# Agent attention with a mixture of experts: two left tiles under way at a time

## The chip, the cores and the metric

The kernel runs on one core of a Trainium2 chip. The metric is the device time of one execution in microseconds (us), the median over several runs. The engines are named as in the profile: PE is the matrix engine (PEld its weight loads), ACT, DVE and POOL are the scalar, vector and general engines, SP issues most of the transfers. SBUF is the on-chip memory from which the engines read, PSUM the small memory of eight banks into which PE writes.

## The reference

Four batches (B = 4) of N = 11456 tokens with C = 128 channels go through an attention by way of 49 agents, and the result, token by token, through the one of E = 8 experts (hidden width F = 1024) that a gate chooses:

```
s1 = softmax(scale * agents @ k.T);  agent_v = s1 @ v
x  = softmax(scale * q @ agents.T) @ agent_v          # N x 128, per batch
e  = argmax(x @ w_gate);  g = softmax(x @ w_gate)[e];  m = sigmoid((x @ w_output_gate)[e])
out = g * m * (relu(x @ w1[e]) @ w2[e])
```

All inputs and outputs are 32-bit floats.

## The kernel before

In each batch one expert has almost all tokens. The **main stream** sends every token of a batch through that expert, in tiles of up to 512 tokens, with 16-bit operands. `mm1` issues a group of eight matmuls `h` (four of its own weights and four of the rest) into PSUM banks 0 to 3; `relu` makes from each bank the two 16-bit parts `hh` (ACT) and `hl` (DVE); `mm2` multiplies them in pairs, one matmul with `hh` and one with `hl`, into a bank `y`; `finish` reads `y` with ACT (`ys`) and DVE (`os`), and `store` writes it out. The matmuls `ks`, `av`, `qs` of the attention, and `lg` of the gate, are put between those of the stream.

The tokens that chose another expert are gathered into **left tiles** of 128 tokens: thirteen from batches 0 to 2 (phase 0) and one from batch 3 (phase 1). They are computed again with their own expert, in 32-bit matmuls, and scattered over the result. `left_prepare` makes the table of tiles and gathers the tokens' attention rows (SP loads of indices, POOL's indirect transfers into `big` or `left_ld`). For each tile, `left_load` loads with SP the agents' values `lav` and the expert's two weight matrices `lw1`, `lw2` of 512 KB each; `left_front` transposes the tokens (`let`, copied by ACT to `let_sb`) and multiplies them with `lav` (`lx`, copied by ACT to `lxs`); `left_back` makes eight matmuls `lh` in two halves of four, each half in one bank and with one ACT relu behind it, then eight matmuls `ly`, and ACT scales the result into its place. A 32-bit matmul shows as two passes in the trace. `left_scatter` then writes the tile with a POOL transfer.

What comes when is settled while the program is built: a planner (class `Clock`) keeps an estimated time for each engine, and the generators (the main stream and the side streams, each with a priority given to `spawn`) hand out their next instruction when the planner thinks its operands ready. `wait_free` asks for a free PSUM bank, `bank` takes the one that is free longest by the planner's time. On the chip every engine works through its list in order and waits on semaphores. Loads of `k`, `q`, `v` and `x` use buffers `ld0` and on (`place` takes one, `scored` gives it back), 128 x 1024 numbers each.

In the kernel before, `left_static` works on one left tile at a time, while the loads and the front of the next one may run ahead:

```
for i, (ph, k) in enumerate(todo):
    while (ph, k) not in ready or i > finished[0] + 1:
        yield None
```

Of the kernel before, what the change touches and what calls it, by code (L numbers as in the profile page):

```python
# [7 lines left out]
F32 = mybir.dt.float32  # L8
# [8 lines left out]
P = 128  # L17
B, N, C, A, E, F = 4, 11456, 128, 49, 8, 1024
A2 = 50
# [233 lines left out]
def agent_attention_top1_moe(ctx, tc, qT, kT, v, aT, wg, wo, w1, w2, cst, out):  # L253
# [245 lines left out]
    def scored(item):  # L499
        places[held.pop(item)][0] = True  # L500
# [92 lines left out]
    def v_weights(b, u):  # L593

        base, pp, nt = UNITS[u]
        S, M = K[b]["S"], K[b]["M"]
        sv = S[0:pp, 8 * u:8 * u + nt, :]

        if b > 0:
            e = wk.tile([P, 8, A2], F32, name=f"ev{b}_{u}", tag="ev", bufs=2)  # L600
        else:
            e = wk.tile([P, 4, C], F32, name=f"ev{b}_{u}", tag="os", bufs=4).rearrange("p t c -> p (t c)")
            e = e[:, 0:8 * A2].rearrange("p (t a) -> p t a", a=A2)
        e = e[0:pp, 0:nt, :]
        yield from (DVE if b == 0 and u % 3 == 0 else POOL).q.tensor_tensor(e, sv, M[0:pp].unsqueeze(1).broadcast_to([pp, nt, A2]), op=ALU.subtract)
        yield from ACT.q.activation(e, e, AF.Exp, scale=SCALE)
        K[b][u] = e
        spawn(v_sum(b, u, e), 1)
# [714 lines left out]
            yield from pause(1500.0 if n > 1 else 0.0)  # L1323
        return ti, tg, ef, oa

    def left_load(ph, ti, k, nm):
        b0, nb, _, _ = PHASES[ph]
        yield from SY.wait(ti)
        er = nc.values_load(ti[0:1, k, 3:4], engines=[SP], min_val=0, max_val=E - 1,
                            skip_runtime_bounds_check_because=WHY)  # L1330
        yield from SY.wait(ti)
        br = nc.values_load(ti[0:1, k, 4:5], engines=[SP], min_val=0, max_val=nb - 1,
                            skip_runtime_bounds_check_because=WHY)
        av = wk.tile([P, C], F32, name=f"lav{nm}", tag="l_av")
        yield from SY.q.dma_start(av[0:A], avnd[b0:b0 + nb][bass.ds(br, 1)].rearrange("a p c -> p (a c)"))
        w1t = wk.tile([P, F], F32, name=f"lw1{nm}", tag="w1t", bufs=2)
        yield from SY.q.dma_start(w1t, w1[bass.ds(er, 1)].rearrange("a p f -> p (a f)"))
        w2t = wk.tile([P, F], F32, name=f"lw2{nm}", tag="w2t", bufs=2)
        yield from SY.q.dma_start(w2t, w2[bass.ds(er, 1)].rearrange("a p f -> p (a f)"))
        return av, w1t, w2t  # L1340

# [6 lines left out]
    def left_front(nm, ef, av):  # L1348
        yield from wait_free()
        t = bank(f"let{nm}")  # L1350
        mark = hold()
        yield from PE.q.transpose(t[0:A, 0:P], ef[:, 0:A], idf)
        et = wk.tile([P, P], F32, name=f"let_sb{nm}", tag="l_et", bufs=1)
        yield from ACT.q.copy(et[0:A], t[0:A, 0:P])
        release(mark)
        yield from wait_free()
        x = bank(f"lx{nm}")
        mark = hold()
        yield from PE.q.matmul(x[:, 0:P], av[0:A], et[0:A], start=True, stop=True)
        xs = wk.tile([P, P], F32, name=f"lxs{nm}", tag="l_xs")  # L1360
        yield from ACT.q.copy(xs, x[:, 0:P])
        release(mark)
        return xs

    def left_back(nm, xs, w1t, w2t, o, ef):
        hidden = []
        for hf in range(2):
            yield from wait_free()
            h = bank(f"lh{nm}_{hf}")
            mark = hold()  # L1370
            for j in range(4):
                fs = slice((4 * hf + j) * P, (4 * hf + j + 1) * P)
                yield from PE.q.matmul(h[:, j * P:(j + 1) * P], w1t[:, fs], xs, start=True, stop=True)
            hs = wk.tile([P, 512], F32, name=f"lh{nm}_{hf}", tag=f"lh{hf}", bufs=1)
            hidden.append(hs)
            yield from ACT.q.activation(hs, h, AF.Relu)
            release(mark)
# [13 lines left out]
                                in_=o, in_offset=None, bounds_check=top - 1, oob_is_err=False)  # L1391

    left = []

    ready = {}

# [18 lines left out]
                    ready[ph, i + k] = t, ti, k, tu[:, k:k + 1], ef[:, k, :], oa[:, k, :]  # L1415
                yield from left_index(ph, i, n, f"s{ph}_{i}", got, big)

    def left_static():
        todo = [(ph, k) for ph, x in enumerate(PHASES) for k in range(x[2])]
        ops = {}  # L1420

        def fronts():
            for i, (ph, k) in enumerate(todo):
                while (ph, k) not in ready or i > finished[0] + 1:
                    yield None
                t, ti, kk, _, ef, _ = ready[ph, k]
                yield from pause(t - clk.now())
                av, w1t, w2t = yield from left_load(ph, ti, kk, f"{ph}_{k}")
                yield from pause(max(clk.ready[x.name] for x in (av, w1t, w2t)) - clk.now())
                xs = yield from left_front(f"{ph}_{k}", ef, av)  # L1430
                ops[ph, k] = xs, w1t, w2t

        finished = [0]
        spawn(fronts(), 4)
        for ph, k in todo:
            while (ph, k) not in ops:
                yield None
            xs = ops.pop((ph, k))
            _, _, _, tu, ef, oa = ready[ph, k]
            yield from left_back(f"{ph}_{k}", *xs, oa, ef)  # L1440
            left.append((ph, oa, tu))
            finished[0] += 1

# [32 lines left out]
    spawn(clear(), 5)  # L1476
    spawn(small_products(), 4)
    spawn(left_prepare(), 1)
    spawn(left_static(), 5)
    spawn(left_scatter(), 3)  # L1480
    main_stream()

# [67 lines left out]
```

## Time and profile before

| what | value |
|---|---|
| median of 3 runs | 1042.22 us (1041.47 to 1042.23) |
| profiled execution | 1041.4 us, span 1039.6 us |
| mean granted clock of PE | 0.997 |
| PE busy | 1018.5 us (98%) |
| PEld busy | 835.1 us (80%) |
| DVE busy | 880.2 us (85%) |
| ACT busy | 589.8 us (57%) |
| POOL busy | 272.9 us (26%) |

The busy times are those of the profiled execution; its own time is 1.8 us longer than its span. All instructions carry the same line number, that of a helper, so that rows are told apart by the names of their operands, in which numbers are left out. PE's busy time counts a matmul from its start to its modelled end, and matmuls overlap.

### The profile page before, as it was taken

The numbers are of one execution on the slowest core, as the hardware profiler recorded it, in microseconds if no ns is written. First come the engines' busy times: TensorE is split into PE (matmuls) and PEld (weight loads), VectorE is DVE, ScalarE is ACT, GpSimd is POOL, SyncE is SP. The second block draws the span as 40 slices with busy tenths as digits, with TensorE's granted clock in tenths as the row PEclk, the third lists the DMA queues.
The fourth block names the chain that finished last, engine by engine and source line by source line (L and its number), as shares of the span: only waits on it lengthen the run. The fifth ranks groups of instructions, "written<-read, shape, count | busy, mean of one in ns | idle before, by whom it ended". The sixth has DMA issues, their size and how long they took to land.

```text
span 1039.6 us, 27765 instructions
## 1 busy us (share of the span) xinstructions
PE 1018.5 (98%) x10690; PEld 835.1 (80%) x10690; DVE 880.2 (85%) x2390; ACT 589.8 (57%) x1396; POOL 272.9 (26%) x442
## 2 busy tenths in 40 slices
PE   9999999999999999999999999999999999999996
PEld 9998877888688878887788888877687687878785
DVE  1748999999998999989998999889999988868851
ACT  1326665656655566565655665565755566565552
POOL 0301323332112222222122232321122333434322
PEclk9999999999999999999999999999999999999998
DMA  8877765544459445453569544444333445442441
GB/s 273 244 181 241 179 134 145 129 139 132 125 139 210 135 127 121 120 165 99 135 159 181 156 124 112 132 146 119 114 101 71 125 97 152 143 134 68 147 145 60
DMA packets 109111, 147.14 MB, mean 142 GB/s; under 512 B 61420, under 2 KB 71840, under 8 KB 108974
## 3 DMA queue, kind: packets, MB, share of 16 engines
q1 hardware_dynamic: 107630, 143.83, 50.8%
q0 software_dynamic: 1344, 1.49, 0.8%
q8 instruction: 85, 1.39, 0.6%
q14 instruction: 52, 0.43, 0.2%
HBM read 91.86 MB, written 35.17 MB: 122 GB/s over the span
## 4 chain that ended last, share of the span: by engine, by line
PE 82%; DVE 13%; ACT 3%; issue 2%; POOL 0%; DMA 0%; POOLq 0%; DVEq 0%; ACTq 0%
PE y L203 40%; PE h L203 17%; DVE hl L203 6%; PE ks L203 6%; PE av L203 6%; PE qs L203 4%; PE lh L203 2%; PE ly L203 2%; ACT hh L203 1%; PE aw L203 1%; PE warm L203 1%; DVE os L203 1%; PE lg L203 1%; DVE ll L203 1%; DVE cum L203 1%
## 5 line engine op out<-in xcount | busy, mean ns | idle before, releaser
L203 PE MATMUL y<-vv,hh 128*128 128x256 f16 (+1 forms) x2880 | 588.3, 273 | 4.7 <-DVE qz L203 3.0
L203 PE MATMUL y<-vv,hl 128*128 128x128 f16 (+1 forms) x2880 | 530.3, 219 | 1.4 <-DVE hl L203 0.7
L203 ACT ACTIVATE hh<-h 128x512 f16<-128x512 f32 (+1 forms) x736 | 372.3, 591 | 203.5 <-PE h L203 203.2
L203 DVE SCALAR_TENSOR_TENSOR hl<-h,hh 128x512 f16<-128x512 f32 (+1 forms) x736 | 446.7, 666 | 44.8 <-ACT hh L203 42.3
L203 PEld LDWEIGHTS <-hh 128*128 128x128 f16 (+1 forms) x2880 | 283.3, 98 | 65.0 <-issue 36.1
L203 PEld LDWEIGHTS <-hl 128*128 128x128 f16 (+1 forms) x2880 | 322.3, 112 | 7.5 <-DVE hl L203 4.0
L203 PE MATMUL h<-x_ld,w 128*128 128x512 f16 (+1 forms) x1472 | 283.9, 376 | 2.4 <-DVE hl L203 1.7
L203 POOL TENSOR_TENSOR os<-os,smt 128x512 f32<-128x512 f32 (+1 forms) x92 | 94.0, 1022 | 299.5 <-issue 224.3
L203 PEld LDWEIGHTS <-w 128*128 128x128 f16 x1472 | 97.2, 103 | 88.7 <-issue 67.5
L203 PEld LDWEIGHTS qs<-at,q_ld 128*128 128x128 f32 x720 | 112.8, 191 | 7.9 <-DVE os L203 0.6
L203 PE MATMUL qs<-at,q_ld 128*128 128x50 f32 x720 | 114.2, 245 | 0.1
L203 ACT COPY ys<-y 128x256 f32<-128x256 f32 x180 | 67.7, 376 | 76.8 <-PE y L203 76.7
L203 PE MATMUL av<-ev,v_ld 128*128 128x50 f32 x720 | 109.7, 251 | 0.0
L203 PEld LDWEIGHTS av<-ev,v_ld 128*128 128x128 f32 x720 | 107.7, 192 | 2.3 <-issue 0.8
L203 PE MATMUL ks<-at,k_ld 128*128 128x50 f32 x720 | 107.9, 256 | 0.4 <-DVE os L203 0.4
L203 PEld LDWEIGHTS ks<-at,k_ld 128*128 128x128 f32 x720 | 104.6, 191 | 2.8 <-DVE os L203 1.6
L203 DVE TENSOR_TENSOR os<-y,ys 128x256 f32<-128x256 f32 x180 | 74.4, 413 | 22.0 <-ACT ys L203 19.3
L203 POOL TENSOR_TENSOR e<-ef,e 128x392 f16<-128x392 f32 (+1 forms) x48 | 41.4, 862 | 156.8 <-ACT e L203 136.6
L203 POOL TENSOR_TENSOR ev<-S,km_o 128x400 f32<-128x400 f32 (+1 forms) x44 | 40.5, 922 | 119.7 <-PE av L203 56.8
L203 PEld LDWEIGHTS <-idle_x 128*128 128x128 f16 x324 | 47.6, 154 | 3.1 <-DVE idle_x L203 1.1
L203 DVE TENSOR_REDUCE m<-ks 128x50 f32<-128x400 f32 (+1 forms) x44 | 23.8, 540 | 25.4 <-ACT S L203 25.0
L203 ACT COPY S<-ks 128x400 f32<-128x400 f32 (+1 forms) x48 | 22.7, 476 | 36.4 <-PE ks L203 36.3
(228 smaller groups left out, 1055.2 us busy)
## 6 DMA issues: line engine op xcount, KB each, us to landing
q_ld<-qT SPq DMA_DIRECT2D x44, 512.0 KB
v_ld<-v SPq DMA_DIRECT2D x44, 512.0 KB
out<-os SPq DMA_DIRECT2D x88, 256.0 KB
k_ld<-kT SPq DMA_DIRECT2D x43, 512.0 KB
lw<-w SPq DMA_DIRECT2D x28, 512.0 KB
efd<-ef SPq DMA_DIRECT2D x44, 200.0 KB
x_ld<-x_ld SPq DMA_DIRECT2D x176, 38.0 KB
w1t<-w SPq DMA_DIRECT2D x8, 256.0 KB
```

The lines of the kernel that those rows point to most:

```text
L203: return getattr(self.eng, op)(*a, **k)
```

## The change

Two generators `left_static(way)` take every other left tile each. A way loads the weights of its next tile only when its previous tile is done. The weights go to the buffers of the loads (`left_place`) and no longer to `w1t` and `w2t`. The second way starts when all values of the last batch are loaded, and its hidden layer lies in the buffers of the tag `ev`, whose shape is made to fit. `let_sb` gets a second buffer.

```diff
@@ -597,7 +597,8 @@
         sv = S[0:pp, 8 * u:8 * u + nt, :]
 
         if b > 0:
-            e = wk.tile([P, 8, A2], F32, name=f"ev{b}_{u}", tag="ev", bufs=2)
+            e = wk.tile([P, 4, C], F32, name=f"ev{b}_{u}", tag="ev", bufs=2).rearrange("p t c -> p (t c)")
+            e = e[:, 0:8 * A2].rearrange("p (t a) -> p t a", a=A2)
         else:
             e = wk.tile([P, 4, C], F32, name=f"ev{b}_{u}", tag="os", bufs=4).rearrange("p t c -> p (t c)")
             e = e[:, 0:8 * A2].rearrange("p (t a) -> p t a", a=A2)
@@ -1323,7 +1324,7 @@
             yield from pause(1500.0 if n > 1 else 0.0)
         return ti, tg, ef, oa
 
-    def left_load(ph, ti, k, nm):
+    def left_load(ph, ti, k, nm, at_=None):
         b0, nb, _, _ = PHASES[ph]
         yield from SY.wait(ti)
         er = nc.values_load(ti[0:1, k, 3:4], engines=[SP], min_val=0, max_val=E - 1,
@@ -1333,9 +1334,15 @@
                             skip_runtime_bounds_check_because=WHY)
         av = wk.tile([P, C], F32, name=f"lav{nm}", tag="l_av")
         yield from SY.q.dma_start(av[0:A], avnd[b0:b0 + nb][bass.ds(br, 1)].rearrange("a p c -> p (a c)"))
-        w1t = wk.tile([P, F], F32, name=f"lw1{nm}", tag="w1t", bufs=2)
+        if at_ is None:
+            w1t = wk.tile([P, F], F32, name=f"lw1{nm}", tag="w1t", bufs=2)
+        else:
+            w1t = yield from at_(f"lw1{nm}")
         yield from SY.q.dma_start(w1t, w1[bass.ds(er, 1)].rearrange("a p f -> p (a f)"))
-        w2t = wk.tile([P, F], F32, name=f"lw2{nm}", tag="w2t", bufs=2)
+        if at_ is None:
+            w2t = wk.tile([P, F], F32, name=f"lw2{nm}", tag="w2t", bufs=2)
+        else:
+            w2t = yield from at_(f"lw2{nm}")
         yield from SY.q.dma_start(w2t, w2[bass.ds(er, 1)].rearrange("a p f -> p (a f)"))
         return av, w1t, w2t
 
@@ -1350,7 +1357,7 @@
         t = bank(f"let{nm}")
         mark = hold()
         yield from PE.q.transpose(t[0:A, 0:P], ef[:, 0:A], idf)
-        et = wk.tile([P, P], F32, name=f"let_sb{nm}", tag="l_et", bufs=1)
+        et = wk.tile([P, P], F32, name=f"let_sb{nm}", tag="l_et")
         yield from ACT.q.copy(et[0:A], t[0:A, 0:P])
         release(mark)
         yield from wait_free()
@@ -1362,7 +1369,7 @@
         release(mark)
         return xs
 
-    def left_back(nm, xs, w1t, w2t, o, ef):
+    def left_back(nm, xs, w1t, w2t, o, ef, tag="lh"):
         hidden = []
         for hf in range(2):
             yield from wait_free()
@@ -1371,7 +1378,7 @@
             for j in range(4):
                 fs = slice((4 * hf + j) * P, (4 * hf + j + 1) * P)
                 yield from PE.q.matmul(h[:, j * P:(j + 1) * P], w1t[:, fs], xs, start=True, stop=True)
-            hs = wk.tile([P, 512], F32, name=f"lh{nm}_{hf}", tag=f"lh{hf}", bufs=1)
+            hs = wk.tile([P, 512], F32, name=f"lh{nm}_{hf}", tag=tag, bufs=2)
             hidden.append(hs)
             yield from ACT.q.activation(hs, h, AF.Relu)
             release(mark)
@@ -1391,6 +1398,8 @@
                                 in_=o, in_offset=None, bounds_check=top - 1, oob_is_err=False)
 
     left = []
+    WAYS, LEFT = 2, 5
 
     ready = {}
 
@@ -1415,29 +1424,41 @@
                     ready[ph, i + k] = t, ti, k, tu[:, k:k + 1], ef[:, k, :], oa[:, k, :]
                 yield from left_index(ph, i, n, f"s{ph}_{i}", got, big)
 
-    def left_static():
-        todo = [(ph, k) for ph, x in enumerate(PHASES) for k in range(x[2])]
+    def left_place(nm):
+        while not vacant():
+            yield None
+        return place((nm, 0, 0), first_place(0, LARGE)[1], [F])
+    def left_static(way):
+        while way and (B - 1 not in K or K[B - 1]["v"] < NU):
+            yield None
+        todo = [(ph, k) for ph, x in enumerate(PHASES) for k in range(x[2])][way::WAYS]
         ops = {}
+        finished = [0]
 
         def fronts():
             for i, (ph, k) in enumerate(todo):
-                while (ph, k) not in ready or i > finished[0] + 1:
+                while (ph, k) not in ready or i > finished[0]:
                     yield None
                 t, ti, kk, _, ef, _ = ready[ph, k]
                 yield from pause(t - clk.now())
-                av, w1t, w2t = yield from left_load(ph, ti, kk, f"{ph}_{k}")
+                av, w1t, w2t = yield from left_load(ph, ti, kk, f"{ph}_{k}", left_place)
                 yield from pause(max(clk.ready[x.name] for x in (av, w1t, w2t)) - clk.now())
                 xs = yield from left_front(f"{ph}_{k}", ef, av)
                 ops[ph, k] = xs, w1t, w2t
 
-        finished = [0]
-        spawn(fronts(), 4)
+        spawn(fronts(), LEFT - 1)
         for ph, k in todo:
             while (ph, k) not in ops:
                 yield None
             xs = ops.pop((ph, k))
             _, _, _, tu, ef, oa = ready[ph, k]
-            yield from left_back(f"{ph}_{k}", *xs, oa, ef)
+            yield from left_back(f"{ph}_{k}", *xs, oa, ef, ("lh", "ev")[way])
+            for x in (f"lw1{ph}_{k}", f"lw2{ph}_{k}"):
+                scored((x, 0, 0))
             left.append((ph, oa, tu))
             finished[0] += 1
 
@@ -1476,7 +1497,8 @@
     spawn(clear(), 5)
     spawn(small_products(), 4)
     spawn(left_prepare(), 1)
-    spawn(left_static(), 5)
+    for way in range(WAYS):
+        spawn(left_static(way), LEFT)
     spawn(left_scatter(), 3)
     main_stream()
 
```

The order that the planner makes of it is the same on every engine up to about 816 us, and the last left tile (phase 1) stands alone behind the last `y` of the main stream in both kernels. In between, the rows of the left tiles stand elsewhere in the same stream. Two places follow. Names end in the tile's number, and the number of a half where there is one; `w` stands for the main stream's first weights, `vv` for its second.

The first place is where the sixth and seventh left tiles (`_5` and `_6`) meet, near 921 us, on PE, now:

```order
L203 MATMUL h_0_3_17389<-x_7_ld,w_0_13705 128x512 [waits DMAHW3_49]
L203 MATMUL qs_11_17383<-at,q_11_ld 96x50
L203 MATMUL lh_6_0_17368<-lxs_6_17354,lw_60_0_ld 128x128 x3
L203 MATMUL ly_5_17388<-lw_50_0_ld,lh_5_0_17327 128x128 [waits DMAHW3_49,DVE_49]
L203 MATMUL ly_5_17388<-lw_50_0_ld,lh_5_0_17327 128x128
L203 MATMUL lh_6_1_17428<-lxs_6_17354,lw_60_0_ld 128x128 [waits Activation_49]
L203 MATMUL lh_6_1_17428<-lxs_6_17354,lw_60_0_ld 128x128 x3
L203 LDWEIGHTS hh_0_17186
L203 MATMUL y_0_17441<-vv_0_13690,hh_0_17186 128x256 [waits Activation_49]
```

Before, behind the same group of `h` on PE:

```order
L203 MATMUL h_0_3_17366<-x_7_ld,w_0_13705 128x512
L203 LDWEIGHTS hh_2_17180
L203 MATMUL y_0_17323<-vv_0_13690,hh_2_17180 128x256
L203 MATMUL lh_5_0_17348<-lxs_5_17333,lw_5_17156 128x128 [waits DMAHW4_49,Activation_49]
L203 LDWEIGHTS hl_2_17181
L203 MATMUL y_0_17323<-vv_0_13690,hl_2_17181 128x128
```

The `lh` and `ly` of two tiles now stand side by side without main matmuls between them, and a new `y` behind them waits for ACT. On ACT the same place reads now:

```order
L203 COPY ys_1_17374<-y_1_17249 128x256 [waits PE_49,Activation_49]
L203 ACTIVATE lh_5_1_17373<-lh_5_1_17342 128x512 [waits PE_49]
L203 ACTIVATE hh_0_17395<-h_0_0_17370 128x512 [waits PE_49]
L203 ACTIVATE hh_1_17398<-h_0_1_17376 128x512 [waits PE_49]
L203 ACTIVATE hh_2_17400<-h_0_2_17385 128x512 [waits PE_49]
L203 ACTIVATE hh_3_17402<-h_0_3_17389 128x512 [waits PE_49]
L203 ACTIVATE lh_6_0_17420<-lh_6_0_17368 128x512 [waits PE_49]
L203 ACTIVATE lh_6_1_17436<-lh_6_1_17428 128x512 [waits PE_49]
```

In the kernel before, the relus of one tile stood there:

```order
L203 COPY lxs_5_17333<-lx_5_17310 128x128 [waits PE_49]
L203 ACTIVATE hh_0_17372<-h_0_0_17350 128x512 [waits PE_49]
L203 ACTIVATE hh_1_17375<-h_0_1_17353 128x512 [waits PE_49]
L203 ACTIVATE hh_2_17377<-h_0_2_17357 128x512 [waits PE_49]
L203 ACTIVATE hh_3_17379<-h_0_3_17366 128x512 [waits PE_49]
L203 ACTIVATE ef_11_17391<-qz_11_17383 96x2x49 [waits DMAHW4_49,DVE_49,Pool_49]
L203 ACTIVATE lh_5_0_17409<-lh_5_0_17348 128x512 [waits PE_49]
L203 CAST e_3_86<-ef_11_17391 96x2x49 [waits DMAHW5_49,Activation_49]
L203 ACTIVATE lh_5_1_17436<-lh_5_1_17416 128x512 [waits PE_49]
```

The relu `lh_6_0` stands directly behind the four `hh` of the group, ahead of the second half's.

The second place is where the ninth and tenth tiles (`_8` and `_9`) meet, near 970 us, on PE, now; ahead of these rows stand, from the `h` group on, eight pairs of `y` with a `pexc` (a small product of the table of tiles) and `let_8` in the first two:

```order
L203 LDWEIGHTS hh_7_18131
L203 MATMUL y_1_18271<-vv_1_13692,hh_7_18131 128x256
L203 LDWEIGHTS hl_7_18132
L203 MATMUL y_1_18271<-vv_1_13692,hl_7_18132 128x128
L203 MATMUL let_9_18351<-kc,big_8_17075 49x128 [waits DMASW6_49,Activation_49]
L203 MATMUL lx_8_18345<-let_sb_8_18326,lav_8_18174 128x128 [waits DMAHW5_49,PE_49]
L203 LDWEIGHTS w_1_13721
L203 MATMUL h_0_0_18358<-x_9_ld,w_1_13721 128x512 [waits DVE_49]
```

The transposition `let_9` stands between two groups of `h`, and waits for ACT; before, one `let` stood further on between `y` pairs, and no second. On ACT, now:

```order
L203 ACTIVATE hh_4_18310<-h_1_0_18296 128x512 [waits PE_49]
L203 ACTIVATE hh_5_18313<-h_1_1_18298 128x512 [waits PE_49]
L203 ACTIVATE hh_6_18315<-h_1_2_18301 128x512 [waits PE_49]
L203 ACTIVATE hh_7_18317<-h_1_3_18304 128x512 [waits PE_49]
L203 COPY let_sb_8_18326<-let_8_18303 49x128 [waits PE_49]
L203 COPY ys_1_18347<-y_1_18271 128x256 [waits DVE_49,PE_49]
L203 COPY let_sb_9_18353<-let_9_18351 49x128 [waits PE_49]
L203 COPY lxs_8_18355<-lx_8_18345 128x128 [waits PE_49]
```

And before:

```order
L203 ACTIVATE hh_4_18289<-h_1_0_18265 128x512 [waits PE_49]
L203 ACTIVATE hh_5_18292<-h_1_1_18267 128x512 [waits PE_49]
L203 ACTIVATE hh_6_18294<-h_1_2_18281 128x512 [waits PE_49]
L203 ACTIVATE hh_7_18296<-h_1_3_18283 128x512 [waits PE_49]
L203 COPY ys_1_18326<-y_1_18238 128x256 [waits DVE_49,PE_49]
L203 ACTIVATE hh_0_18369<-h_0_0_18352 128x512 [waits PE_49]
```

The copies of the two transpositions now stand behind `hh_4` to `hh_7`, and `let_9` takes the bank that `let_sb_8` reads.

## Rows read from the trace of the kernel before

**Rows 1.** The page: the span, and the chain of waits by engine.
```profile
span 1039.6 us, 27765 instructions
...
PE 82%; DVE 13%; ACT 3%; issue 2%; POOL 0%; DMA 0%; POOLq 0%; DVEq 0%; ACTq 0%
```

**Rows 2.** Stretches: length; busy PE, PEld, DVE, ACT, POOL; clock, DMA share, GB/s.
```profile
836.00:1025.00 189.00, 189.00 (x1888) 155.90 (x1887) 143.41 (x419) 106.35 (x258) 66.75 (x89) 1.00 0.42 126
1025.00:1040.00 15.00, 5.04 (x41) 4.42 (x39) 0.49 (x2) 2.53 (x7) 2.67 (x3) 0.81 0.04 12
```

**Rows 3.** Groups of PE from 836 to 1025 us: count, busy, mean, idle.
```profile
L203 PE MATMUL y<-vv,hh 128*128 128x256 f16 (+1 forms) x541 | 113.9, 273 | 0.0
...
L203 PE MATMUL h<-x_ld,w 128*128 128x512 f16 (+3 forms) x264 | 51.7, 374 | 0.0
L203 PE MATMUL ly<-lw,lh 128*128 128x128 f32 x208 | 40.1, 275 | 0.0
L203 PE MATMUL lh<-lxs,lw 128*128 128x128 f32 x200 | 38.7, 275 | 0.0
```

**Rows 4.** Timeline of PE near 915 us: start, duration, engine, instruction.
```profile
914.94 1.35 PE L203 MATMUL h<-x_ld,w 128*128 128x512 f16 x8
916.23 0.28 PE L203 MATMUL y<-vv,hh 128*128 128x256 f16 x1
...
917.23 0.27 PE L203 MATMUL y<-vv,hh 128*128 128x256 f16 x1
...
917.50 0.27 PE L203 MATMUL y<-vv,hh 128*128 128x256 f16 x1
...
917.66 0.27 PE L203 MATMUL y<-vv,hh 128*128 128x256 f16 x1
...
918.99 0.27 PE L203 MATMUL y<-vv,hh 128*128 128x256 f16 x1
...
921.78 0.27 PE L203 MATMUL y<-vv,hh 128*128 128x256 f16 x1
...
922.17 0.27 PE L203 MATMUL y<-vv,hh 128*128 128x256 f16 x1
```

**Rows 5.** Timeline near 835 us; in brackets idle time and releaser.
```profile
834.63 0.60 ACT L203 ACTIVATE lh<-lh 128x512 f32<-128x512 f32 x1 [0.27 <-PE lh L203]
...
835.28 0.27 PE L203 MATMUL y<-vv,hh 128*128 128x256 f16 x1 [0.54 <-ACT lh L203]
```

**Rows 6.** Timeline of PE and ACT near 921 us.
```profile
921.38 0.28 PE L203 MATMUL y<-vv,hh 128*128 128x256 f16 x1
...
921.48 2.06 ACT L203 ACTIVATE hh<-h 128x512 f16<-128x512 f32 x4 [1.50 <-PE h L203]
...
923.57 0.60 ACT L203 ACTIVATE lh<-lh 128x512 f32<-128x512 f32 x1
```

**Rows 7.** Timeline of PE and ACT near 970 us.
```profile
968.45 1.35 PE L203 MATMUL h<-x_ld,w 128*128 128x512 f16 x8
...
969.83 2.06 ACT L203 ACTIVATE hh<-h 128x512 f16<-128x512 f32 x4 [1.94 <-PE h L203]
...
971.75 0.41 ACT L203 COPY ys<-y 128x256 f32<-128x256 f32 x1
...
976.57 0.25 ACT L203 COPY let_sb<-let 49x128 f32<-49x128 f32 x1
```

**Rows 8.** Timeline of PE at the end.
```profile
1025.33 0.27 PE L203 MATMUL let<-kc,bigs 128*49 128x128 f32 x1
...
1028.85 2.05 PE L203 MATMUL ly<-lw,lh 128*128 128x128 f32 x16
```

**Rows 9.** Timeline of SP and PE near 1005 us.
```profile
1001.80 4.46 SPq L203 DMA_DIRECT2D lw<-w  x2
...
1009.03 0.39 PE L203 MATMUL lh<-lxs,lw 128*128 128x128 f32 x2
```

## The prediction

> **What bounds the kernel now.** I read four views of the profile, in this order. First the page and the division of the span into stretches by what the order of instructions shows: before 816 us nothing moves on any engine, the left tiles fill the stretch from 836 us to the last matmul of the main stream, and one left tile stands alone behind that. [rows 1] give the span, 1039.6 us, and a chain that is 82% PE. [rows 2] say what matters: from 836 to 1025 us PE is busy for 189.00 us of 189.00 at a granted clock of 1.00 (2.4 GHz), while DVE has 143.41, ACT 106.35 and POOL 66.75. No matmul there waits for anything; the 15 us behind it are a chain of one tile, with 5.04 us of PE.
>
> A busy PE need not be PE at its peak, so second I ask whether those 189 us hide waits between overlapping matmuls. Distances between starts tell it, with the counts in [rows 3] and the timeline in [rows 4]. Eight y pairs (hh and hl) take 918.99 − 917.66 = 1.33 us, 0.166 us a pair; 541 pairs make 89.9 us. A group of eight h matmuls takes 916.23 − 914.94 = 1.29 us; 264 are 33 groups, 42.6 us. A y pair with two lh passes inside takes 922.17 − 921.78 = 0.39 us, so the two passes cost 0.224; (208 + 200)/2 such pairs make 45.7 us. A let inside a pair takes 917.50 − 917.23 = 0.27, so it costs 0.10. Together 178.2 us, and 10.8 us remain for the 135 other small matmuls of the 1888, 0.08 us each, which is what such rows cost. So the stretch is the sum of its matmuls, each at its steady distance: there is no idle time for a second tile to fill, and matmuls of two left tiles cost the same 0.224 us a pair wherever they are put.
>
> A rule of the Trainium skill speaks against reading it that way: its page "Perfetto Trace Analysis", section "Identifying the Most-Contended Engine", says that matmul busy time is a poor measure of headroom because matmuls overlap, and that the busy share of weight loads is a better one. By that, PE's 155.90 us of weight loads in 189.00 would leave 33.1 us open, and a change that brings more independent matmuls could take some of them. The sum of starts above bears the rule out only so far as busy time alone proves nothing; the starts leave next to none. I give it a rival below.
>
> Third, the end [rows 8]: the last left tile's let starts at 1025.33 us, straight behind the main stream; ly starts at 1028.85 and the span ends 14.3 us after the let. In the changed order the same rows (let, lx, lh, ly) stand alone behind the last y, so none of this is taken away by the change.
>
> **The change part by part.** *Counts.* Every instruction is still issued once: no matmul, copy or transfer is added or removed. Cost 0.
>
> *Two tiles under way.* The tiles' matmuls change places in a PE stream without gaps: 0 by the sum above. The thirteenth tile, the last of the first three batches, ends some 50 main matmuls earlier, which nothing waits for, because the last tile still follows the stream. What can cost is a PE instruction that now waits for something nearer than before. I looked for places where a matmul takes over a PSUM bank from a tile whose ACT work stands behind a row of hh relus. The trace of before has one of this kind [rows 5]: a y takes the bank of the first lh half, whose relu ends at 834.63 + 0.60 = 835.23; the y starts at 835.28 after 0.54 us of idle PE. The handover is 0.05 us. That place is the same in both kernels: 0. The changed order has two new ones.
>
> Place A, between the sixth and seventh tile (near 921 us): behind an h group come a qs, three passes of lh_6_0, then ly_5, four rows of lh_6_1, and then a new y that takes the bank of lh_6_0. Call the end of the h group T0. In [rows 6] the y behind such a group starts at 921.38 = T0; ACT's four hh run from 921.48 for 2.06 us, and the lh relu behind them starts at 923.57 and takes 0.60. It ends at T0 + 2.79, the y could start at T0 + 2.84. In front of the y PE has one qs (0.1, as the small matmuls above) and nine lh and ly matmuls of two passes, 9 × 0.224 = 2.02: T0 + 2.12. Wait: **+0.72 us**. Bounds: 0, if the relu finds ACT free before the fourth hh (ACT is in order and the relu is queued behind all four, so I put little on it), and 1.3 if another ACT instruction of a relu's length (0.60) gets ahead of it.
>
> Place B, between the ninth and tenth tile (near 970 us): let_9 takes the bank of let_8, whose copy let_sb_8 stands on ACT behind hh_4 to hh_7. In [rows 7] the h group starts at 968.45, T0 = 968.45 + 1.29 = 969.74; the four hh start at 969.83 and ACT's next instruction starts at 971.75, T0 + 2.01. A let_sb takes 0.25, so the bank is free at T0 + 2.26, let_9 at T0 + 2.31. Ahead of let_9 PE has eight y pairs (1.33), let_8 (0.10) and a small pexc (0.1): T0 + 1.53. Wait: **+0.78 us**. Lower bound 0, if PE reaches that group later than ACT does.
>
> Every other bank in the changed order that passes from a left tile to a y has at least two more main pairs or an h group ahead of it: 0. The relus of a second tile also delay hh and hl on ACT by 0.60 us each; ACT has 82 us free in the stretch and hh lie several groups ahead of their y: 0, and up to 0.6 us at a place if not.
>
> *Weights in the load buffers, no load ahead.* Before, a tile's loads start as soon as the tile two ahead of it is finished; now too, since each way waits for its own previous tile while the other way works. In [rows 9] the two weight loads of a tile are issued from 1001.80 over 4.46 us and the first lh starts at 1009.03, 7.2 us later: 2.8 us beyond the issue. I take 0. Upper bound: the time from a let to its ly, when nothing else is between, is 1028.85 − 1025.33 = 3.5 us [rows 8], against 4.46 us of issue; if a tile's let goes with its first load and its ly follows at that pace, the ly is early by 1.0 us, and PE, in order, waits that long, per tile. The wait of the second way for the values' loads, and the v_weights temporaries in a new shape, are over before 836 us: 0.
>
> **Sum** against the profiled execution (span 1039.6 and 1.8 around it): 1041.4 + 0.72 + 0.78 = 1042.9 us. It lies 0.8 us under the median of the runs, 1042.22; on that basis 1043.7. I put the forecast between the two, 1043.3 us, 1.1 us or 0.1% over the median. A difference of 0.2%, 2.08 us, is about what a measurement of this kernel can tell from no change.
>
> **The rivals.** *Hidden:* ACT finishes earlier relative to PE than in the rows I used and both new waits vanish; the time stays 1042.2 us. For it speaks that in the 189 us of [rows 2], with relus of left tiles all the way, PE never waited; against it that both places have four hh ahead on an engine that works in order.
>
> *Slower:* two tiles fall into phase, as at place A, where ly_5 and lh_6 stand side by side, so four weight loads queue on SP one behind the other and a tile's second load arrives late. One such tile costs 1.0 us, with the two waits 1042.2 + 1.5 + 1.0 = 1044.7 us, two 1045.7; it decides as soon as the tiles' lateness passes 2.08 − 1.5 = 0.6 us. For it speaks the 4.46 us of issue in [rows 9], against it the 7.2 us of lead.
>
> *Faster:* there is room inside PE's busy time after all, and two independent tiles let PE close it. A tenth of the 33.1 us between PE's and the weight loads' busy time in [rows 2] gives 1042.2 − 3.3 = 1038.9 us. That is the rule of the Trainium skill above at work; against it stands the sum of starts. The change not doing what it says for the end (the last tile still alone behind the stream) is already in my sum.
>
> **How the numbers follow.** Two short waits 0.55; hidden 0.15; slower 0.22; faster 0.08. The likeliest gives 1043.3. The range takes in the slower case with one or two late tiles, and on the lower side the spread of the runs: 1041.0 to 1045.8. Slower by over 2.08 us means above 1044.3: 0.22. Faster means under 1040.1: 0.08. Within: 0.70.
>
> **What would show it.** Right: PE in 836 us to the end of the stream is idle for 0.5 to 0.9 us once near 921 with a y waiting for an ACT lh, and once near 971 with a let waiting for ACT let_sb; the last y ends 1 to 2 us later, and the last let follows it directly, with 14 us behind it. Wrong: an lh or ly that waits for a DMA of lw; PE waits at more than these two places; or starts of y pairs that are closer than 0.166 us in stretches where two tiles are mixed.

## The result, and the profile after

The changed kernel takes 1050.42 us (median of 5, 1050.14 to 1054.85), the one before 1042.23 us in the same series. The ratio is 1.0086, 95% interval 1.0071 to 1.0101: 8.2 us slower, where 1.1 us were forecast, and outside the range. The page of the profiled execution (1050.14 us), beside [rows 1]:

```profile
span 1048.3 us, 27744 instructions
...
PE 1022.4 (98%) x10690; PEld 835.6 (80%) x10690; DVE 884.3 (84%) x2390; ACT 590.4 (56%) x1396; POOL 272.4 (26%) x442
...
PE 79%; DVE 14%; ACT 3%; issue 2%; DMA 1%; POOL 0%; DVEq 0%; POOLq 0%; ACTq 0%
```

PE's counts are the same, the chain has 3 points less of PE and 1 more of DVE. The stretches, with the columns of [rows 2]:

```profile
836.00:1025.00 189.00, 184.42 (x1790) 148.81 (x1789) 144.73 (x411) 104.61 (x251) 64.25 (x87) 0.99 0.41 121
1025.00:1049.00 24.00, 13.66 (x139) 12.54 (x137) 2.97 (x12) 5.06 (x14) 4.72 (x5) 0.91 0.19 64
970.00:980.00 10.00, 7.34 (x51) 4.87 (x49) 8.73 (x21) 4.81 (x13) 1.04 (x1) 0.83 0.53 153
...
976.00:979.00 3.00, 3.00 (x24) 2.48 (x20) 2.25 (x4) 2.19 (x5) 0.00 (x0) 0.54 0.24 36
979.00:982.00 3.00, 3.00 (x19) 1.73 (x17) 0.90 (x4) 0.92 (x4) 1.08 (x2) 0.89 0.05 15
```

PE's waits from 836 us to the last let (what waited, for whom; us in total, times, longest; pptsb is a copy for the table of left tiles):

```profile
PE h L203 <- DVE hl L203: 3.5, 8, 2.0
PE lh L203 <- ACT pptsb L203: 0.5, 1, 0.5
PE y L203 <- ACT lh L203: 0.3, 1, 0.3
PE lh L203 <- ACT lxs L203: 0.2, 1, 0.2
```

PE, which never waited in this stretch before, is idle for 4.6 of 189 us. The main wait is one that the prediction had at nothing: h groups wait for DVE's hl, which must free their banks. Near 970 us the granted clock is 0.83 on average. It is 1.00 from 970 to 976 us, 0.54 from 976 to 979 and 0.89 from 979 to 982: behind the longest wait PE ran for (3 x 0.46 + 3 x 0.11) / 0.5 = 3.4 us at 1.2 GHz, the lower of its two levels, and then at 2.4 GHz again. What all this costs is read by setting the start of each main matmul beside that of the same matmul before, less the left tiles' rows at their steady distance:

| stretch of the main stream (time in the trace after) | later than before, us | the same for a second pair of traces (below) |
|---|---|---|
| up to 836 us | 0.2 | -0.5 |
| 836 to 861: an lh behind ACT | 0.5 | 0.5 |
| 861 to 874: h group behind hl | 1.2 | 1.2 |
| 874 to 911 | -0.1 | -0.3 |
| 911 to 916: h behind hl | 0.4 | 0.0 |
| 916 to 946: place A, lh of two tiles | 0.9 | 0.9 |
| 946 to 968 | 0.0 | 0.0 |
| 968 to 989: h group behind hl, place B, an lh | 5.7 | 3.2 |
| 989 to the last y | 0.0 | 0.0 |
| the last y (the parts are rounded) | 8.7 | 5.0 |

The last left tile comes straight behind the stream, as in [rows 8], with 14.3 us from its let to the end:

```profile
1034.01 0.27 PE L203 MATMUL let<-kc,bigs 128*49 128x128 f32 x1
```

**The largest place.** Timeline near 970 us, all engines together (start, duration; in brackets idle time and releaser):

```profile
964.28 2.06 ACT L203 ACTIVATE hh<-h 128x512 f16<-128x512 f32 x4 [1.41 <-PE h L203]
969.39 0.37 ACT L203 COPY ys<-y 128x256 f32<-128x256 f32 x1 [3.05 <-PE h L203]
...
969.80 0.42 DVE L203 TENSOR_TENSOR os<-y,ys 128x256 f32<-128x256 f32 x1 [2.40 <-ACT ys L203]
970.14 2.83 DVE L203 TENSOR_TENSOR_SCAN cum<-ones,oht 128x90 f32<-128x90 f32 x8
972.88 2.45 DVE L203 SCALAR_TENSOR_TENSOR hl<-h,hh 128x512 f16<-128x512 f32 x4
...
970.31 1.04 POOL L203 TENSOR_TENSOR os<-os,smt 128x512 f32<-128x512 f32 x1 [1.61 <-DVE os L203]
...
973.60 0.38 PE L203 MATMUL h<-x_ld,w 128*128 128x512 f16 x1 [1.99 <-DVE hl L203]
974.20 0.38 PE L203 MATMUL h<-x_ld,w 128*128 128x512 f16 x1 [0.22 <-DVE hl L203]
```

Three things stand one behind the other. ACT is free at 966.34, and the last matmul of the y that ys copies, from 966.12 on, has ended by then, but ys starts at 969.39 (the fifth series comes back to this). DVE's os waits for it; behind os stand the eight scans (cum, one for each expert, which count its tokens for the table of left tiles) of the last batch, 2.83 us, and only then the hl of the group. So the next h starts at 973.60, 1.99 us late, and each of the next three again waits 0.22 us for one hl.

**The second place**, near 868 us:

```profile
865.78 1.83 DVE L203 TENSOR_TENSOR ld<-ll,lm 128x64 f32<-128x64 f32 x1
...
867.78 2.48 DVE L203 SCALAR_TENSOR_TENSOR hl<-h,hh 128x512 f16<-128x512 f32 x4
...
866.49 1.03 POOL L203 TENSOR_TENSOR os<-os,smt 128x512 f32<-128x512 f32 x1
...
868.52 0.38 PE L203 MATMUL h<-x_ld,w 128*128 128x512 f16 x1
869.12 0.38 PE L203 MATMUL h<-x_ld,w 128*128 128x512 f16 x1 [0.22 <-DVE hl L203]
```

DVE's ld, a subtraction of 128 x 64 numbers in the computation of the gate (ll, lm, ld, lr and rm are its steps), takes 1.83 us. It ends at 867.61, just behind POOL's multiplication of a result by the gate (os), which ends at 867.52. In the kernel with that multiplication cut short (below) the same ld takes 0.33 us. The hl behind it come late, and the h group with them.

**The predicted places.** A, timeline of all engines near 928 us:

```profile
926.99 1.06 PE L203 MATMUL lh<-lxs,lw_ld 128*128 128x128 f32 x8
927.63 1.12 ACT L203 ACTIVATE lh<-lh 128x512 f32<-128x512 f32 x2
...
928.31 0.27 PE L203 MATMUL y<-vv,hh 128*128 128x256 f16 x1 [0.26 <-ACT lh L203]
```

The y could have started at 926.99 + 8 x 0.112 = 927.88 and started at 928.31: 0.43 us. B falls into the stretch of the lower clock, and is read in a second trace of the changed kernel, taken later on another chip (fifth series below):

```profile
974.42 0.22 PE L203 MATMUL y<-vv,hl 128*128 128x128 f16 x1
974.91 0.27 ACT L203 COPY let_sb<-let 49x128 f32<-49x128 f32 x1
...
975.23 0.31 PE L203 MATMUL let<-kc,big 128*49 128x128 f32 x1 [0.59 <-ACT let_sb L203]
```

The last y ahead of the let started at 974.42, a let follows one 0.06 later, and it started at 975.23: 0.75 us.

### The profile page after: what moved, and what is told of

It is laid out like the page before. It is cut to its first block, busy times and chain, and to the rows that moved or that the text cites. A ratio compares the mean times of both kernels' runs of the same rounds, so it can differ in the third digit from the quotient of the medians.

```text
span 1048.3 us, 27744 instructions
## 1 busy us (share of the span) xinstructions
PE 1022.4 (98%) x10690; PEld 835.6 (80%) x10690; DVE 884.3 (84%) x2390; ACT 590.4 (56%) x1396; POOL 272.4 (26%) x442
## 4 chain that ended last, share of the span: by engine, by line
PE 79%; DVE 14%; ACT 3%; issue 2%; DMA 1%; POOL 0%; DVEq 0%; POOLq 0%; ACTq 0%
PE y L203 38%; PE h L203 16%; DVE hl L203 7%; PE ks L203 6%; PE av L203 6%; PE qs L203 4%; PE ly L203 2%; PE lh L203 2%; ACT hh L203 2%; PE aw L203 1%; DVE os L203 1%; PE warm L203 1%; DVE cum L203 1%; PE lg L203 1%; DVE ll L203 1%
```

## The experiments

Each ran with a profile and was timed in turns with the kernel before on the same chip; ratios are to that kernel, with a 95% interval. They came in five series, each on one chip.

**First series: parts and shifts.** One way with load ahead (`WAYS, LEFT = 1, 5`, and in `fronts`):

```diff
-                while (ph, k) not in ready or i > finished[0]:
+                while (ph, k) not in ready or i > finished[0] + (WAYS == 1):
```

> One way (WAYS = 1) that loads its next tile ahead, all else as changed: the weights in the load buffers are then the only part of the change that is left. Theory 1 (the time is lost where DVE work stands ahead of the hl of a group while PE runs the pure main stream, so that an h group waits for its bank): the second way matters only by where it moves the stream against DVE's side work; this kernel should be free of the 971 us wait if its scans stand in another place, 1041 to 1045 us. Theory 2 (two tiles side by side cost PE by themselves): 1042.2 us, plus or minus 1. Theory 3 (weights in the load buffers hold up the loads): stays near 1050 us.

1047.84 us, 1.0039 (1.0025 to 1.0053). So the load buffers alone, with another order, cost half as much as the change. In the trace the last y comes 3.6 us later than before, and the last let, which waits for its tokens, another 2.3 us. Then the scans in pairs (in `q_tail`):

```diff
         for e in range(E):
+            if b == B - 1:
+                yield from pause(1500.0)
             yield from DVE.q.tensor_tensor_scan(...)
```

> The changed kernel with the eight scans of the last batch (cum) in pairs, a planner's pause ahead of each, and nothing else; the order is the same up to the scans. Theory 1: the 2.2 us and 3 x 0.4 us waits of the h group at 971 us go, and with them the half clock behind them, 5 to 5.6 us in all: 1044.8 to 1045.4 us. Theory 2: the scans are a symptom, another place gives the wait back: 1049 to 1051 us.

1052.51 us, 1.0082 (1.0059 to 1.0105). The loss near 971 us fell from 5.7 to 2.7 us, but the table of the last batch, made from the scans, came later, and the last let now waited 1.9 us for its tokens behind the stream. Neither theory had that. The kernel before, and the changed one, with a shift:

```diff
-                yield from pause(t - clk.now())                                # kernel before
+                yield from pause(t - clk.now() + (1000.0 if i == 0 else 0.0))
-        spawn(fronts(), LEFT - 1)                                              # changed kernel
+        yield from pause(2000.0 if way else 0.0)
+        spawn(fronts(), LEFT - 1)
```

> The kernel before, with its first left tile started 1 us of planner's time later; no other edit, nothing that should cost. Theory 1: the order against DVE's side work is drawn anew, and the time may move by one or more such waits: 1041 to 1048 us, with each wait of an h group for hl, or its absence, seen in the trace. Theory 2: 1042.2 us, plus or minus 0.8.

> The changed kernel, the second way started 2 us of planner's time later. Theory 1: the order behind 836 us is drawn anew; the loss of 8.2 us changes by several us, up or down, with the waits of h groups for hl. Theory 2 (two ways as such): 1049 to 1052 us.

1054.26 us, 1.0104 (1.0087 to 1.0120), and 1051.54 us, 1.0078 (1.0061 to 1.0095). A shift of 1 us in the kernel before, with one way and the old buffers, costs as much as the whole change. Its trace has eight short waits of h for hl, and behind the stream:

```profile
1036.35 0.42 PE L203 MATMUL let<-kc,bigs 128*49 128x128 f32 x1 [4.11 <-SPq L1485]
```

**Second series: the same order with one suspect out of the way.** The scans moved behind four hl in DVE's list, all else in place (in `run`, `f` being the call itself):

```diff
-        return getattr(self.eng, op)(*a, **k)
+        if any(x.name.startswith("cum3") for x in outs) or (any(x.name.startswith("cum3") for x in ins) and "dma" in op):
+            BEHIND.append(f)
+            return None
...
+        r = f()
+        if BEHIND and outs[0].name.startswith("hl"):
+            COUNT[0] += 1
+            if COUNT[0] == 4:
+                while BEHIND:
+                    BEHIND.pop(0)()
+        return r
```

> The changed kernel with every engine's order kept, except that DVE's eight scans of the last batch stand behind the four hl of the group that they stood ahead of, not ahead. Theory 1 (DVE work ahead of the hl makes the h group wait for its bank): of the 5.6 us lost near 971 us, 4 to 5 come back; what stays is the 1.2 us by which ACT's hh of that group start late, and the short wait of the second let: 1045.2 to 1046.4 us. Theory 2 (two tiles as such, the scans being only a symptom): 1049.5 to 1050.5 us.

POOL's multiplication cut (in `emit`), alone and with the moved scans:

```diff
+        if self.name == "POOL" and op == "tensor_tensor" and outs[0].name.startswith("os"):
+            a = [x[:, :, 0:8] for x in a]
```

> The changed kernel with every engine's order kept; POOL's multiplication of the result by the gate (os) works on 8 of 128 channels only, so the scaling is left out for the others. Theory 1a (DVE operations on SBUF that meet it last until it ends, 1.83 instead of 0.22 us at 865.78, 1.16 instead of 0.32 at 970.39, and so hold the hl back): the h waits at 868 go (1.2 us) and the one at 971 gets shorter by about 0.8 us: 1047.5 to 1048.5 us, a little less if the earlier batches win too. Theory 1b (the length of such DVE operations has another reason): they stay at 1.8 and 1.2 us, and the time at 1050.4 us.

> Both edits of the two kernels before this one together, order kept. Theory 1 with 1a: the gains add, all but the 0.2 to 0.7 us waits at 851, 921, 927 and 983 us and the late hh at 971 us: 1043.0 to 1045.0 us. If one of the edits only uncovers another wait: no better than the better one of the two alone.

> The kernel before with its first left tile started 2 us of planner's time later, after 1 us gave 1054.26 us. Theory 3 (the order of the kernel before is a lucky draw among many, and any shift of the left tiles loses it): again well over 1042.2 us, 1045 to 1055 us. If the loss of the 1 us shift was an accident of its own: 1041 to 1044 us.

1045.64 us, 1.0040 (1.0026 to 1.0054); 1034.34 us, 0.9937 (0.9920 to 0.9953); 1035.32 us, 0.9946 (0.9929 to 0.9963); 1051.26 us, 1.0095 (1.0078 to 1.0112). The cut multiplication gave far more than the 2 to 3 us that were expected, since earlier batches win too: at 812 us its main stream is already 9.5 us ahead of the kernel before. Moving the scans as well gave nothing more, and against the expectation the gains did not add; in both kernels with moved scans a pexc now waits 1.1 us for tot, which is made from them. The 2 us shift again lost 10 us, this time because two left tiles stayed behind the stream and the last let waited 4.8 us.

**Third series: the POOL multiplication in both kernels, and another form of it.** The kernel before with the cut, then four operations with one number a partition (and the same four on ACT, as `activation(..., AF.Copy, scale=...)`):

```diff
+            o, x, s = a
+            for j in range(o.shape[1]):
+                self.eng.tensor_scalar(o[:, j, :], x[:, j, :], s[:, j, 0:1], None, op0=k["op"])
+            return None
```

> The kernel before, order kept, POOL's multiplication of the result by the gate on 8 of 128 channels only (the scaling of the others is left out). If the holds of DVE by this POOL operation are what the changed order met and the one before avoided, then with both kernels freed of it the 8.2 us between them shrink to the bank waits that remain, 1.5 to 2.0 us: the changed kernel so cut took 1034.3 us where before took 1040.9, so this one takes 1032 to 1033 us. If the holds cost both kernels alike and the loss is elsewhere, the 8.2 us stay: 1026 us.

> The kernel before, order kept, each POOL multiplication of 512 by a spread gate as four of 128 by one number a partition (the same result). If DVE waits only for the POOL operation under way, a hold of 1.03 us becomes one of some 0.3 to 0.4: about half of the 9 us that the cut multiplication gives come back, 1035 to 1039 us. If the hold lasts as long as POOL has work, or four operations take longer in sum: 1041 to 1045 us.

> The changed kernel with the same edit, order kept (the same result). With short holds: half of the 15 us of the cut multiplication, 1038 to 1044 us, and the difference to the kernel before so edited is 2 to 5 us. If the hold isn't shortened: 1049 to 1052 us.

> The kernel before, order kept, the same multiplication as four operations on ACT, put into ACT's list where POOL's stood (the same result). POOL then no longer holds DVE, as in the cut multiplication (some 9 us to gain); but ACT's hh stand behind 4 operations of some 0.25 us: up to 1 us on 92 tiles, hidden where hh has over 1 us. 1034 to 1040 us if mostly hidden, over 1045 us if the hh become late.

1032.97 us, 0.9924 (0.9907 to 0.9942); 1033.28 us, 0.9924 (0.9906 to 0.9942); 1035.46 us, 0.9945 (0.9927 to 0.9963); on ACT 1063.05 us, 1.0220 (1.0197 to 1.0244), since ACT's hh became late: the operations took 398 ns each there, and DVE stood idle for hh before hl for 103.7 us in place of 42.3. Freed of this multiplication the two kernels differ by 1034.34 - 1032.97 = 1.4 us, or 2.2 us with the four operations. The second of these kernels leaves nothing out and is 7.6 us faster than before.

The traces say where each gain lies. The mark is the start of the main-stream matmul that starts at 812.01 us in the kernel before; up to it nothing has moved in any of these kernels (times in us):

| kernel | mark | last y | between |
|---|---|---|---|
| before, two traces | 812.01, 811.64 | 1025.27, 1025.04 | 213.3, 213.4 |
| changed, two traces | 812.17, 811.19 | 1033.95, 1030.02 | 221.8, 218.8 |
| before, multiplication cut | 802.87 | 1016.12 | 213.3 |
| changed, multiplication cut | 802.55 | 1017.51 | 215.0 |
| before, four operations | 803.92 | 1017.66 | 213.7 |
| changed, four operations | 804.11 | 1019.61 | 215.5 |

Behind the mark the kernel before gains nothing: there its order met no hold that cost time, and its whole gain comes from the batches ahead, where the two kernels are alike. The changed kernel gains 3.3 to 3.8 us behind the mark against its second trace. The 1.7 or 1.8 us by which it stays longer are about the three bank waits that hang on ACT: A with 0.43, B with 0.75 and the lh behind pptsb with 0.5.

My reason for the four operations was wrong: they are no shorter pieces of the same hold. POOL's group in the kernel before (count, busy time, mean ns):

```profile
L203 POOL TENSOR_TENSOR os<-os,smt 128x512 f32<-128x512 f32 (+1 forms) x92 | 94.0, 1022 | 299.5 <-issue 224.3 <-DVE os L203 23.0 <-DVE sm L203 21.5
```

And in the kernel before with four operations:

```profile
L206 POOL TENSOR_SCALAR os<-os,smt 128x128 f32<-128x128 f32 x360 | 216.2, 613 | 199.9 <-DVE os L208 154.7 <-issue 24.7 <-DVE rm L208 7.5
```

DVE's ll, which reads two operands from SBUF, in the changed kernel (second trace):

```profile
L203 DVE TENSOR_TENSOR ll<-lL,rr 128x128 f32<-128x128 f32 (+1 forms) x48 | 22.2, 463 | 0.8
```

And in the changed kernel with four operations:

```profile
L208 DVE TENSOR_TENSOR ll<-lL,rr 128x128 f32<-128x128 f32 (+1 forms) x48 | 14.8, 310 | 0.8
```

Four operations of 613 ns take more than twice POOL's time, and still ll falls from 463 to 310 ns. So the form decides (two operands against one and a number a partition), and not the length. A little of the hold is left: the longest scan in this trace takes 0.53 us in place of 0.32.

**Fourth series: is it the same cause in other orders?** The four operations in the shifted kernels and in one way, order kept:

> The kernel before with its first left tile 1 us later (1054.26 us as such), order kept, and each POOL multiplication as four operations with one number a partition. If the holds of DVE are also what makes one order of the left tiles so much worse than another: the 6.7 us by which its main stream ended later than that of the kernel before fall under 2 us; the wait of the last tile for its data behind the stream stays: 1036 to 1041 us. If shifted orders lose for other reasons: 1044 to 1047 us, 11 us over the kernel before with the same edit (1033.28).

> The changed kernel with its second way 2 us later (1051.54 us as such), order kept, with the same edit. If the holds are the cause: 1034 to 1037 us, as the changed kernel with it (1035.46). If not: 1041 to 1046 us.

> One way with the weights in the load buffers (1047.84 us as such), order kept, with the same edit. If the holds are the cause of the 3.6 us in its main stream: that shrinks to under 1.5 us, the last tile's wait for data of 2.3 us stays: 1035 to 1039 us. If not: 1039 to 1042 us.

1039.40 us, 0.9962 (0.9950 to 0.9975); 1037.15 us, 0.9944 (0.9927 to 0.9961); 1037.22 us, 0.9951 (0.9933 to 0.9969). Against 1.0104, 1.0078 and 1.0039 all three gained 0.9 to 1.4%, more than the 0.8% of the kernel before. The five orders lay within 1.04% with the old form and lie within 0.38% with the new one, each as a ratio on its own chip.

This shows less than it seems to. From the mark to the last y the first kernel went from 219.4 to 216.9 us, the second from 223.4 to 217.2, the third only from 217.1 to 216.5. Against the 213.7 of the kernel before with the edit, 2.8 to 3.5 us stay in each, where under 2 and under 1.5 were expected of the first and the third; the second came out over its 1037 us. The time by which the last let comes late behind the stream, which was to stay, fell from 4.8 and 2.3 us to 1.4 and 1.3 in these two, and helped their totals. So the hold explains a part of what these orders cost, little of it in the third, and the rest is open; all six traces also have the late signals of the next series.

**Fifth series: the same chip for before, changed and moved scans.** Setting the traces side by side showed something that no theory had. In those of the first and fourth series, and in the first trace of the changed kernel, PE's semaphore is updated late at six to thirteen places, though its matmuls run on; the ys at 969.39 is one (no update from 964.36 to 969.37, then ten within 0.40 us). In those of the second and third series there is next to none, and in the two of the kernel before there is one each.

> The kernel before itself, for a second trace on the chip of the next two. In some of the traces PE's signals (the updates of its semaphore) come late by 0.6 to 4.7 us while its matmuls run on; in the profile of the kernel before one does. Theory A: such late signals are a matter of the chip that the run falls on, so this trace shows many if those of the next two do; ratio 1.000.

> The changed kernel itself. Theory A (late signals of PE cost part of the 8.2 us, the 3.0 us late copy ys at 969.39 above all): on a chip without them the place near 971 us loses about 2 us in place of 5.6, and the ratio to before is 1.003 to 1.005; on a chip with them it is 1.007 to 1.010 again. Theory B (the order alone): 1.007 to 1.010 on any chip.

> The changed kernel with the eight scans behind the four hl. Theory B (the scans ahead of the hl cost most of the 5.6 us at 971 us): 0.4 to 0.5% faster than the changed kernel on the same chip. Theory A: within 0.2% of it where the trace shows no late signals, and where it does, the hl no longer wait for the scans, so that up to 0.3% is won.

1041.22 us, 0.9999 (0.9990 to 1.0009); 1046.67 us, 1.0053 (1.0039 to 1.0067); 1044.80 us, 1.0036 (1.0022 to 1.0050). This chip shows no late signal in the changed kernel, and the change costs 5.5 us, not 8.2, as theory A had it; its trace has no stretch at the lower clock near 970 us either (granted clock 1.00 from 970 to 980 us). PE's waits in that trace, from 836 us to the last let:

```profile
PE h L203 <- DVE hl L203: 1.6, 7, 0.3
PE let L203 <- ACT let_sb L203: 0.6, 1, 0.6
...
```

The place near 970 us, timeline of ACT, DVE, POOL and PE:

```profile
964.95 0.37 ACT L203 COPY ys<-y 128x256 f32<-128x256 f32 x1
967.12 2.06 ACT L203 ACTIVATE hh<-h 128x512 f16<-128x512 f32 x4 [1.80 <-PE h L203]
...
966.21 3.62 DVE L203 TENSOR_TENSOR_SCAN cum<-ones,oht 128x90 f32<-128x90 f32 x8
969.75 1.85 DVE L203 SCALAR_TENSOR_TENSOR hl<-h,hh 128x512 f16<-128x512 f32 x3
...
967.38 1.06 POOL L203 TENSOR_TENSOR os<-os,smt 128x512 f32<-128x512 f32 x1
...
970.47 0.38 PE L203 MATMUL h<-x_ld,w 128*128 128x512 f16 x1 [0.30 <-DVE hl L203]
```

Now ys follows the hh at once and the scans start 0.33 us behind os; but they take 3.62 us, since a POOL multiplication meets them at 967.38: one scan lasts 1.95 us in place of 0.32 (with the scans moved the eight took 1.99), and PE still stands idle 0.3 us before the first h and 0.22 before each of three more. Moving the scans saves 1.9 us here by the medians, 0.7 by the spans of the two traces, with intervals that overlap, and brings the wait of pexc: of the 4.8 us that seemed won in the second series, most was the other chip.

## Why the prediction was wrong, point by point

- *No idle time to win in the stretch, the tail not taken away:* right. No second tile filled anything. The rule of the Trainium skill ("Perfetto Trace Analysis", "Identifying the Most-Contended Engine"), taken as a rival, gave nothing here: pairs of y behind B's group still start 0.16 to 0.17 us apart. The last let follows the stream at once.
- *Counts; weights late:* the counts are the same; no lh or ly waits for a load of lw in either trace. The rival that was slower by late weights had the sign and not the mechanism.
- *Place A, 0.72 us:* 0.43. With T0 at 925.61, the start of the qs behind the h group, ACT's relu ended at T0 + 2.65 in place of 2.79, and PE's own work took 2.28 in place of 2.12, the qs alone 0.2 in place of 0.1. *Place B, 0.78 us:* 0.75. Both waits exist where and why they were put.
- *"ACT has 82 us free in the stretch and hh lie several groups ahead of their y: 0"* is the step that failed. It weighed hh and hl against the y that read them, and not against the next h group, which needs the banks that hl frees, and it had no term for what else stands ahead of the hl on DVE. Where no left tile lies between, an h group starts every 4.27 us (958.63, 962.90 and 967.16 in the changed kernel). Behind the second of these the four hl run from 964.91 to 967.39, as soon as hh lets them; the first h of the next group starts at 967.16, the fourth, 3 x 0.22 later, at 967.82. So 0.4 us is all that DVE has there, and if its hl begin 1 us later, PE waits. Left tiles' matmuls stretch these intervals. The change moved them away from the gate's DVE work of two batches, and at two places that work met a POOL multiplication: 1.2 us at 868, and 1.6 of the 3.2 us near 970 (in the second trace the group of eight h took 972.89 - 970.47 = 2.42 us in place of 1.29, three distances of 0.60 in place of (3 x 0.60 - 1.13) / 3 = 0.22, and it began 0.46 late, behind an hl matmul of 969.95 that the next one follows by 0.06 elsewhere). Freed of that multiplication, 1.4 to 2.2 us of the 5.5 stay. So the term at 0 was worth some 3.5 us. The prediction had named the sign: PE waits at more than its two places. PE's waits of the changed kernel with four operations, from 820 to 1020 us:

```profile
PE y L208 <- ACT lh L208: 0.8, 2, 0.5
PE let L208 <- ACT let_sb L208: 0.6, 1, 0.6
PE lh L208 <- ACT pptsb L208: 0.5, 1, 0.5
PE h L208 <- DVE hl L208: 0.2, 1, 0.2
```

h's waits for hl are gone but for one of 0.2 us; those that hang on ACT stay: a y for an lh, 0.3 us at A (the other is that of [rows 5], in both kernels); B; and an lh behind pptsb, 0.5 us, which the sum had at nothing too.
- *"The forecast between the profiled execution and the median"* left out that the same kernel differs from chip to chip. The first trace of the changed kernel lost 2.9 us more than the second at the places of late signals (0.4 at 913, 2.5 near 970, the stretch at the lower clock among it). In the first and fourth series the kernel before took 1043.2 and 1043.1 us, against 1040.9 to 1041.2 on the chips without them; that late signals are the reason is not shown, since it has no trace there. On either chip the result lies above the range, so the step above failed without them too.
- *The order of the kernel before as a typical one:* the premise under all of it. A 1 us or 2 us shift of its first left tile cost 10 to 11 us, and the other two orders tried lost too. What they lost lies in part in the same holds, in part in a wait of the last let behind the stream (4.8 us after both shifts), and in part it is open.

What makes PE's signals late is open: the traces of one series are alike, but a series is one chip and one time, and no edit was made that tells more. The cases that the prediction priced inside its range sum to 0.55 + 0.15 + 0.22 = 0.92, and it gave the range 0.70; the rest had no name, and the cause that came was in it.

## What to carry to other kernels

Where a built-in planner fixes every engine's order, price a change not by its own waits only, but by what any other order costs: shift something harmless by a microsecond first and time that. Read the slack of an in-order helper from the next use of the bank that it frees, not from the next use of its result. And when DVE rows of one shape differ several times in length, look at what POOL does in that microsecond; here the form of one POOL operation was worth as much as a change of order, 7.6 us in the kernel before and about 11 in the changed one (1046.67 - 1035.46, two chips).

## What the runs showed of the hardware

- DVE operations with two operands in SBUF that met POOL's two-operand multiplication lasted until it ended, 0.1 to 0.2 us behind it (ld 1.83 us in place of 0.33, and 416 ns on average in place of 222 with four operations; ll 463 in place of 310). Those with one were not held: hl, with its other operand in PSUM, kept 666 ns, and the reduction lm took 207 against 205 ns. The Trainium skill's page "SBUF — State Buffer", section "Who interferes with whom", says that a DVE instruction with two SBUF inputs contends with a GpSimd instruction that reads SBUF. The traces agree for the two-operand form of POOL's operation. For its other form, which reads SBUF too, they show next to nothing of it: ld took 222 ns beside the four operations and 226 with the multiplication cut, ll 310 and 290. The held ld (865.78) and the held scan (966.70) had begun 0.7 us before the multiplication's recorded start; what held them at first is not shown.
- PE's semaphore updates came up to 4.7 us late in some traces, in bursts, while its matmuls ran on; the ys of the largest place waited 3.05 us for one.
- PE idle time undercounts such losses: the h matmuls that start 0.60 us apart in place of 0.22 lose 0.38 each, and 0.22 of that shows as idle.
